# Attention, FFN and gated convolution on one core: the low halves of q and k are subtracted on VectorE instead of GpSimd

## The chip, the cores and the metric

One Trainium2 chip, one of its cores. The metric is the device time of one execution in microseconds (us). The engines have in-order instruction streams: TensorE (PE in the profile, its weight loads PEld), VectorE (DVE), ScalarE (ACT), GpSimd (POOL) and SyncE (SP, which here issues every DMA).

## The reference

Batch 4, 12 heads, sequence 448, head size 64, model width 768, FFN width 3072, all fp32:

```python
scores = scale * q @ k.T - log(S); attn = 1 / (1 + exp(-scores)); x = attn @ v
u = x + real(fft(fft(x, axis=1), axis=2))          # over sequence and width
un = (u - mean(u)) / sqrt(var(u) + 1e-6)
y = u + relu(un @ w_ch1) @ w_ch2
gate = sigmoid(causal_conv5(y)); out = (gate * (y @ w_val)) @ w_out
```

## The kernel before

Every product that needs more than one short-mantissa pass is split in a high and a low half: x = h + l, and a product is taken as three matmuls, h·h, h·l and l·h. For q and k this is done on the chip, in `halves_of` (lines 302 to 310): the high half h is x rounded to fp32r, written by ScalarE (line 308) or, for the first pairs, by VectorE (line 306); the low half l is x − h, one tensor_tensor on GpSimd (line 309).

The attention works on 24 pairs of heads (4 batches of 6). A pair has q of 128 × 448 and k of 128 × 512 (k's last 64 columns are laid out twice, with zeros, so that the fourth tile of keys takes both heads in one matmul). The loop of lines 640 to 695 has 96 passes, t = 0 to 95, four for each pair, one per tile of 128 keys. The order in which a pass issues its work is the order of the code, and each engine keeps it; nothing reorders it:

- `scores(t + 1)` on TensorE (lines 355 and 357), from qh, ql, kh, kl of its pair; it runs one pass ahead. The first score tile of the next pair is thus issued in the pass with t % 4 == 3.
- `sigmoid(t)` on ScalarE.
- In the pass with t % 4 == 0, `prep_q` of the next pair, in the pass with t % 4 == 1 `prep_k`: the high half on ScalarE behind the sigmoid, the low half on GpSimd. The diff touches the second of these. There are 24 ql and 24 kl. Below, ql(t) and kl(t) are those issued in pass t.
- Loads of later q, k, v by SP, and with t % 4 == 2 a maximum over v (line 104, VectorE).
- One step of the background queues, whose VectorE and ScalarE work is issued behind the halves of this pass: `fq`, the Fourier stage of the batch before (lines 400 to 552: sums and differences of x on VectorE, halves ph and pl for the first transform's matmuls of line 464, halves zh and zl of its result for the matmuls of line 481, and additions of the outcome to acc, lines 489 and 492); `lq`, the normalisation of the batch before that (lines 558 to 626); `wq`, the preparation of FFN weights (line 181 on: bit operations on VectorE that turn loaded 64-bit floats into fp32, then maxima and halves). ScalarE work of these queues goes through `push` and `drain` and comes at the pass's end.
- `values(t − 1)` on TensorE (lines 380 and 382), and the copy of a finished pair to acc (line 389).

After the attention, the last batches' Fourier and normalisation run beside the first FFN blocks (`up`, `down`), then come the FFN over eight groups of weights, the gate, and two projections. None of these uses `halves_of`. They have GpSimd work of their own (lines 230, 599, 834), which the diff leaves alone.

Of the kernel before, what the change touches and what calls it, by code (L numbers as in the profile page):

```python
# [7 lines left out]
F32 = mybir.dt.float32  # L8
# [5 lines left out]
ALU = mybir.AluOpType  # L14
# [46 lines left out]
def body(tc, qd, kd, vd, w1d, w2d, cwd, wvd, wod, cdd, k12d, csd, eyed, out):  # L61
    nc = tc.nc
    V, A, P = nc.vector, nc.scalar, nc.gpsimd
# [238 lines left out]
    def halves_of(x, nm, n, on_v):  # L302
        h = wk.tile([128, n], F32R, tag=nm + "h", bufs=2, name=nm + "h")
        l = wk.tile([128, n], F32R, tag=nm + "l", bufs=2, name=nm + "l")
        if on_v:
            V.tensor_copy(h, x)
        else:
            A.activation(out=h, in_=x, func=AF.Copy)
        P.tensor_tensor(out=l, in0=x, in1=h.bitcast(F32), op=ALU.subtract)
        return h, l  # L310

    def prep_q(i):
        qk[i] = halves_of(raw[i][0], "q", S, i == 0)

    def prep_k(i):
        qk[i] += halves_of(raw.pop(i)[1], "k", 512, i < 3)
# [746 lines left out]
```

## Time and profile before

| | |
|---|---|
| time, median of 3 runs | 1081.48 us (1080.37 to 1082.52) |
| profiled execution | 1081.04 us |
| its span, first to last instruction | 1079.2 us |
| mean granted TensorE clock | 0.995 |
| busy: PE, DVE, ACT, POOL | 1058.7, 739.2, 444.4, 180.3 us |

Busy time counts what an engine executes, not what it waits for. The page gives the busy time in whole; the chain that ended last lies in the projections at the end, since every stage hands on to the next. A row of the timeline reads: start, duration, engine, line, operation, output<-inputs, shape, count of merged instructions, and in brackets how long the engine stood idle just before and what ended that.

### The profile page before, as it was taken

To read this page: it belongs to the slowest core of one execution; us is meant where nothing else is said; L and a number is where in the kernel's file an instruction comes from. 1 tells how busy PE (TensorE), PEld (TensorE's weight loads), DVE (VectorE), ACT (ScalarE), POOL (GpSimd) and SP (SyncE) were. 2 spreads that over 40 slices of the span, in tenths; PEclk is the share of its full clock that TensorE was granted. 3 is DMA by queue.
4 is the path that set the end of the run, shared out by engine and by line. 5 is a ranking of instruction groups with operands and counts; after the bars stand their busy time and mean duration, and the time that the engine had idled before them with its cause. 6 is when DMAs were issued, how large, how long until landed. Compare 5 with 4: busy or idle time off the path is not lost. (4 is left out here: it accounts for less than half of the span.)

```text
span 1079.2 us, 15323 instructions
## 1 busy us (share of the span) xinstructions
PE 1058.7 (98%) x5616; PEld 548.9 (51%) x5616; DVE 739.2 (68%) x2143; ACT 444.4 (41%) x686; POOL 180.3 (17%) x162
## 2 busy tenths in 40 slices
PE   9999999999899999999999999999999999999998
PEld 5345454546455555555555555555555545555554
DVE  2866999696985666667676566666666787776530
ACT  5675757732232233333233333133333374444321
POOL 3322223200020112211021122012221061000000
PEclk9999999999999999999999999999999999999999
DMA  6632432011112322223322222322222200000001
GB/s 218 211 94 88 130 97 88 11 46 45 30 30 59 83 64 69 78 60 88 89 75 72 60 74 72 89 73 60 73 71 76 60 1 1 1 35 35 35 35 69
DMA packets 34780, 74.13 MB, mean 69 GB/s; under 512 B 3940, under 2 KB 11920, under 8 KB 34704
## 3 DMA queue, kind: packets, MB, share of 16 engines
q1 hardware_dynamic: 34704, 73.15, 23.7%
q8 instruction: 44, 0.72, 0.3%
q14 instruction: 32, 0.26, 0.1%
HBM read 67.46 MB, written 5.51 MB: 68 GB/s over the span
## 5 line engine op out<-in xcount | busy, mean ns | idle before, releaser
L730 PE MATMUL ps_s<-un,w1hi 128*128 128x448 f16 x1152 | 312.8, 353 | 2.0 <-DVE hl L739 2.0
L753 PE MATMUL ps_m<-hh,w2hi 128*128 128x448 f16 x576 | 203.5, 353 | 3.6 <-DVE acc L757 2.4
L753 PE MATMUL ps_m<-hh,w2lo 128*128 128x448 f16 x576 | 203.6, 353 | 0.0
L753 PE MATMUL ps_m<-hl,w2hi 128*128 128x448 f16 x576 | 203.4, 353 | 0.0
L730 PE MATMUL ps_s<-un,w1lo 128*128 128x448 f16 x576 | 203.4, 353 | 0.0
L753 PEld LDWEIGHTS <-w2hi 128*128 128x128 f16 x1152 | 112.4, 98 | 109.4 <-issue 5.0
L730 PEld LDWEIGHTS <-w1hi 128*128 128x128 f16 x1152 | 112.9, 98 | 108.3 <-issue 4.1
L757 DVE SCALAR_TENSOR_TENSOR acc<-ps_m,rg,acc 128x448 f32<-128x448 f32 x192 | 129.1, 680 | 36.8 <-PE ps_m L753 36.6
L178 ACT ACTIVATE wabs<-w 128x384 f32<-128x384 f32 (+1 forms) x109 | 58.4, 547 | 223.9 <-DMA w<-w2d 81.1
L739 DVE SCALAR_TENSOR_TENSOR hl<-ps_s,hh 128x896 f16<-128x896 f32 x64 | 54.7, 855 | 80.0 <-ACT hh L737 79.9
L189 DVE TENSOR_SCALAR_CACHE_REDUCE wabs<-wabs 128x192 f32<-128x192 f32 (+1 forms) x234 | 74.7, 354 | 41.7 <-ACT wabs L178 40.7
L368 ACT ACTIVATE sg<-ps_s,logb 128x896 f32<-128x896 f32 x96 | 86.5, 912 | 26.8 <-PE ps_s L355 22.6
L753 PEld LDWEIGHTS <-w2lo 128*128 128x128 f16 x576 | 56.4, 98 | 53.0 <-issue 0.7
L730 PEld LDWEIGHTS <-w1lo 128*128 128x128 f16 x576 | 56.5, 98 | 52.8 <-issue 0.4
L191 DVE TENSOR_SCALAR wf<-wabs 128x192 int32<-128x192 int32 (+1 forms) x234 | 54.4, 272 | 35.6 <-POOL w1lo L230 13.2
L929 PE MATMUL ps_m<-xs,wvhi 128*128 128x448 f16 x288 | 78.0, 352 | 0.0
L197 DVE SCALAR_TENSOR_TENSOR wf<-w,wf 128x192 int32<-128x192 int32 (+1 forms) x234 | 77.3, 369 | 0.3
L737 ACT ACTIVATE hh<-ps_s 128x896 f16<-128x896 f32 x64 | 46.1, 720 | 73.6 <-PE ps_s L730 73.6
L194 DVE SCALAR_TENSOR_TENSOR wf<-w,wf 128x192 int32<-128x192 int32 (+1 forms) x234 | 74.6, 357 | 0.3
L380 PE MATMUL ps_m<-sg,v 128*64 128x448 f32 x288 | 70.3, 568 | 0.0
L810 DVE SCALAR_TENSOR_TENSOR gp<-acc,cw,gp 128x448 f32<-128x448 f32 x72 | 49.3, 685 | 20.3 <-ACT gp L808 18.4
L954 PE MATMUL ps_m<-gh,wohi 128*128 128x448 f16 x144 | 50.8, 352 | 0.0
(185 smaller groups left out, 1399.1 us busy)
## 6 DMA issues: line engine op xcount, KB each, us to landing
w<-w1d SPq DMA_DIRECT2D x42, 384.0 KB
w<-w2d SPq DMA_DIRECT2D x42, 384.0 KB
k<-kd SPq DMA_DIRECT2D x24, 256.0 KB
v<-vd SPq DMA_DIRECT2D x24, 256.0 KB
q<-qd SPq DMA_DIRECT2D x24, 224.0 KB
out<-o SPq DMA_DIRECT2D x24, 224.0 KB
w<-wvd SPq DMA_DIRECT2D x12, 384.0 KB
w<-wod SPq DMA_DIRECT2D x12, 384.0 KB
```

Source lines behind the costliest of these rows:

```text
L178: A.activation(out=wa, in_=z[:, :, 1].bitcast(F32), func=AF.Abs)
L189: V.tensor_scalar(out=a, in0=a, scalar1=LEAST, scalar2=None, op0=ALU.max, op1=ALU.max, accum_out=m[:, i:i + 1])
L191: V.tensor_scalar(out=f.bitcast(I32), in0=a.bitcast(I32), scalar1=0x07FFFFFF, scalar2=3, op0=ALU.bitwise_and, op1=ALU.logical_shift_left)
L194: V.scalar_tensor_tensor(out=f.bitcast(I32), in0=lo, scalar=29, in1=f.bitcast(I32), op0=ALU.logical_shift_right, op1=ALU.bitwise_or)
L197: V.scalar_tensor_tensor(out=f.bitcast(I32), in0=hi, scalar=-0x40000000, in1=f.bitcast(I32), op0=ALU.bitwise_and, op1=ALU.bitwise_or)
L368: A.activation(out=sg[:, :n], in_=sc.pop(t)[:, :n, :S], func=AF.Sigmoid, scale=1.0 / math.sqrt(D), bias=logb)
L380: nc.tensor.matmul(p[hs, :S], v[:, s, hs], a[:, h], start=(s == 0), stop=False)
L730: nc.tensor.matmul(p[:, i, :S], w[:, k, fs], u[:, k], start=(m == 0), stop=(m == 17))
L739: V.scalar_tensor_tensor(out=l[:, :nf], in0=p[:, :nf, :S], scalar=0.0, in1=h[:, :nf], op0=ALU.max, op1=ALU.subtract)
L753: nc.tensor.matmul(p[:, :S], w[:, f, js], hh[f // 2][k][:, f % 2], start=(m == 0), stop=(m == 3 * FC - 1))
L757: V.scalar_tensor_tensor(out=acc[b][:, j, PAD:], in0=p[:, :S], scalar=rg, in1=acc[b][:, j, PAD:], op0=ALU.mult, op1=ALU.add)
L929: nc.tensor.matmul(p[:, :S], w[:, k, js], u[:, k], start=(n == 0), stop=(n == 17))
```

## The change

One line: the subtraction that makes the low half is issued on VectorE's stream in place of GpSimd's. Operands, shapes, place in the code and everything around it are the same.

```diff
@@ halves_of
             V.tensor_copy(h, x)
         else:
             A.activation(out=h, in_=x, func=AF.Copy)
-        P.tensor_tensor(out=l, in0=x, in1=h.bitcast(F32), op=ALU.subtract)
+        V.tensor_tensor(out=l, in0=x, in1=h.bitcast(F32), op=ALU.subtract)
         return h, l
```

## Rows read from the trace of the kernel before

**Rows 1.** The page, busy time and share of each engine.
```profile
PE 1058.7 (98%) x5616; PEld 548.9 (51%) x5616; DVE 739.2 (68%) x2143; ACT 444.4 (41%) x686; POOL 180.3 (17%) x162
```

**Rows 2.** Busy time by stretch: stretch, length, PE, PEld, DVE, ACT, POOL; clock, DMA.
```profile
105.00:148.00 43.00, 41.87 (x220) 19.81 (x220) 41.94 (x85) 29.41 (x44) 14.05 (x11) 1.00 0.43 127
164.00:196.00 32.00, 30.14 (x156) 13.56 (x152) 31.12 (x60) 23.92 (x36) 9.95 (x8) 1.00 0.25 74
232.00:300.00 68.00, 60.62 (x323) 34.59 (x322) 57.74 (x159) 19.42 (x29) 2.75 (x3) 0.95 0.14 36
```

**Rows 3.** Line 309: duration min/median/max in ns; what ended POOL's idle time.
```profile
L309 POOL TENSOR_TENSOR ql<-q,qh x24: 1135/1144/1957, 3.8 to 202.3; 128x448 fp32r<-128x448 f32 x24
L309 POOL TENSOR_TENSOR kl<-k,kh x24: 1265/1284/1703, 5.3 to 208.4; 128x512 fp32r<-128x512 f32 x24
  ACT qh L308: 88.5, 22
```

**Rows 4.** DVE groups of 105 to 148 us: operation, shapes, count, busy us, mean ns.
```profile
L104 DVE TENSOR_REDUCE vm<-v 128x1 f32<-128x512 f32 x5 | 3.4, 678 | 0.0
L398 DVE TENSOR_TENSOR pm<-acc 128x448 f32<-128x448 f32 x2 | 1.1, 611 | 0.0
```

**Rows 5.** Timeline, 25 to 37 us: passes 7 to 15.
```profile
25.16 0.69 DVE L181 TENSOR_SCALAR wabs<-w 128x256 int32<-128x256 int32 x1 [9.70 <-DMA w<-w1d]
...
26.01 0.36 PE L355 MATMUL ps_s<-qh,kl 64*128 64x448 f32 x2
...
27.13 0.42 DVE L197 SCALAR_TENSOR_TENSOR wf<-w,wf 128x256 int32<-128x256 int32 x1
...
36.27 0.47 PE L355 MATMUL ps_s<-qh,kh 64*128 64x448 f32 x2 [1.90 <-ACT sg L368]
```

**Rows 6.** Timeline, 66 to 93 us: passes 32, 33, 41 and 42.
```profile
66.56 0.68 DVE L450 SCALAR_TENSOR_TENSOR e<-eo,st,e 12x452 f16<-12x452 f32 x1
67.29 0.92 DVE L436 SCALAR_TENSOR_TENSOR pl<-pm,st,ph 128x678 f16<-128x678 f32 x1
68.05 0.56 ACT L308 ACTIVATE qh<-q 128x448 fp32r<-128x448 f32 x1
70.04 0.66 PE L464 MATMUL ps_m<-cd,pl 128*113 128x385 f16 x3
90.64 0.63 ACT L308 ACTIVATE kh<-k 128x512 fp32r<-128x512 f32 x1
91.78 0.62 DVE L456 SCALAR_TENSOR_TENSOR zl<-ps_m,rt,zh 112x385 fp32r<-112x385 f32 x1 [4.54 <-ACT zh L259]
92.44 0.09 PEld L481 LDWEIGHTS ps_m<-cs,zl 112*6 112x6 f32 x1 [0.38 <-DVE zl L456]
```

**Rows 7.** Passes 45 to 62: the stretch 99.5 to 104.3, then timeline rows.
```profile
99.50:104.30 4.80, 4.80 (x32) 2.74 (x29) 4.13 (x17) 1.97 (x4) 0.00 (x0) 1.00 0.16 48
...
103.66 0.63 ACT L308 ACTIVATE kh<-k 128x512 fp32r<-128x512 f32 x1
...
109.03 2.76 DVE L564 TENSOR_TENSOR tt<-tt,acc 128x448 f32<-128x448 f32 x3
...
113.11 0.37 PE L355 MATMUL ps_s<-qh,kl 64*128 64x448 f32 x2
...
136.38 1.05 DVE L585 TENSOR_TENSOR tt<-tt 128x448 f32<-128x448 f32 x1
...
138.15 0.95 PE L596 MATMUL ps_m<-ones,tt 128*112 128x1 f32 x8 [0.18 <-DVE tt L587]
```

**Rows 8.** Timeline, 148 to 174 us: passes 65, 66 and 72.
```profile
148.46 0.63 ACT L308 ACTIVATE kh<-k 128x512 fp32r<-128x512 f32 x1
...
151.10 0.28 PE L481 MATMUL ps_m<-cs,zl 112*6 112x256 f32 x1
...
171.89 0.37 PE L355 MATMUL ps_s<-qh,kl 64*128 64x448 f32 x2
...
172.31 1.95 DVE L564 TENSOR_TENSOR tt<-tt,acc 128x448 f32<-128x448 f32 x3
```

## The prediction, as put on record before the run

> **What bounds the kernel now.** I read the busy times first. TensorE is busy 98% of the span, VectorE 68%, GpSimd 17% [rows 1]: an engine that is relieved here gains nothing by itself, and what counts is only whether TensorE gets its operands earlier or later. Next the busy times by stretch. The diff acts in the attention alone, and there the averages mislead: from 105 to 148 us VectorE is busy 41.94 of 43 us and from 164 to 196 us 31.12 of 32, while TensorE loses 1.13 and 1.86 us [rows 2]. In these stretches VectorE is as full as TensorE. Then line 309: GpSimd takes 1.14 us for a ql and 1.28 for a kl, and waited 88.5 us for qh in 22 of its 24 ql [rows 3]. It does nothing else there, so each low half starts the moment its high half is out, and whatever VectorE is doing. Last the timeline, beside the code's order of issue, for the question that a share of busy time can't answer: where VectorE's stream stands when the high half comes. That decides, because on VectorE the subtraction has a place in a queue: if VectorE is early it must wait there for ScalarE, with everything queued behind; if it is late, TensorE waits for the subtraction.
>
> **What goes and what comes.** 24 ql and 24 kl leave GpSimd. On VectorE the nearest row is the fp32 tensor_tensor of line 398, two SBUF inputs, 128 × 448, 0.611 us, and for 512 columns 0.68 (the reduction of line 104 over 128 × 512 takes 0.678) [rows 4]. Added: 24 × 0.61 + 24 × 0.68 = 31 us of VectorE work. The bounds are these and GpSimd's own durations, which would make 58; the operation of the same kind on the same engine is the nearer row.
>
> Something comes back. Three chained tensor_tensors of line 564 take 1.95 us at 172.31, but 2.76 at 109.03, where GpSimd runs a ql [rows 7, 8]; line 585 takes 1.05 at 136.38 in place of 0.61 [rows 4, 7]. VectorE instructions that meet line 309 on GpSimd are held up, and that ends. From 104.8 to 138 us there are seven such, the first in these rows 0.8 and the last 0.4, together about 5.2 us. So in the full stretches the work on VectorE stays about level. What doesn't stay is the order, and the sum is made of that, place by place. The cost at each is how much later TensorE gets what it already waits for, or gets just in time.
>
> *Passes 7 to 9 (late).* VectorE stands 9.70 us for a load of weights until 25.16; kl(9) lies behind the conversion that follows, whose last instruction ends at 27.13 + 0.42 = 27.55 [rows 5]. With ql(8) at 0.6 in between and 0.6 of hold-ups gone, kl(9) ends at 27.55 + 0.68 = 28.2. TensorE reads it at 26.01: 2.2 us late. TensorE then idles 1.90 before 36.27, for a sigmoid that sits behind a load [rows 5]; that load isn't moved, so this idle time covers 1.9. Left: 0.3. Without the cover it is 2.2.
>
> *Passes 32 and 80 (early).* VectorE would come to ql(32) at 66.5 and wait for qh, which ends at 68.05 + 0.56 = 68.61. Behind it stand line 450 (0.68) and pl (0.92), so pl ends at 68.61 + 0.61 + 0.68 + 0.92 = 70.8; TensorE takes it at 70.04 [rows 6]. 0.8 us; the same three stand behind ql(80). Together 1.6.
>
> *Passes 41, 65 and 89 (early).* kh(41) ends at 90.64 + 0.63 = 91.27. Then kl 0.68, the first zl 0.62, line 104 0.68, the second zl 0.62: 93.87, where TensorE's weight load now waits for it until 92.44 [rows 4, 6]. 1.4 us. The same chain of 2.6 us follows two more times; there it has 2.0 us, from 148.46 + 0.63 = 149.09 to 151.10 [rows 8]: 0.6 each. Together 2.6.
>
> *Pass 45 and the full stretch.* kh(45) ends at 103.66 + 0.63 = 104.29, kl(45) at 104.97. Between 99.5 and 104.3 VectorE did 4.13 us of work [rows 7] that is queued behind kl(45) in the code. So it is 4.8 us late at the start of a stretch in which it has 1.1 us to spare [rows 2]. The first to feel it is kl(49), wanted at 113.11. Up to 138 come four ql and three kl, 4.5 us; the hold-ups give 5.2 back, idle time some 0.7: 4.8 + 4.5 − 5.2 − 0.7 = 3.4. At 138.15 TensorE starts a matmul that waited for VectorE [rows 7], so all of it arrives: 3.4 us. Bounds: nothing, if the hold-ups give twice as much, and 4.8.
>
> *Pass 73.* kl(73) is queued behind the first of the line 564 instructions that start at 172.31, but TensorE reads kl at 171.89 [rows 8]: even on the old schedule VectorE gets there too late, by 172.31 + 0.65 + 0.68 − 171.89 = 1.8, plus its lateness from kl(69) and less the hold-ups. Bounds 0 and 4.8; I take 2.0.
>
> Sum: 0.3 + 1.6 + 2.6 + 3.4 + 2.0 = 9.9 us. Between these places VectorE waits for ScalarE again, which is shifted with TensorE, so the terms add; what falls inside one full stretch I counted once. After the attention TensorE is idle 7.4 us of 232 to 300, but VectorE is busy 57.74 of the 68 [rows 2]: that idle time ends on VectorE, which is shifted too, and covers nothing. From 300 us on nothing is touched. The profiled execution took 1081.04 us, 0.44 under the median: 1081.04 + 9.9 = 1090.9, and 1091 against the median.
>
> **The rivals.** *Faster:* the hold-ups are what counts. If VectorE's results reach TensorE earlier for that, most of what TensorE loses in the two full stretches goes, 1.13 + 1.86 = 3.0 us [rows 2], and the time is 1078. It decides where VectorE is late and no low half is wanted soon. For it: a VectorE subtraction is half of GpSimd's [rows 3, 4], and the full stretches get about as much back as they get in. Against it: three of the places above are early waits, which no shorter instruction removes, and kl(9) and kl(73) stand behind work that TensorE doesn't need.
>
> The Trainium skill speaks for this rival: GPSIMD Engine Reference, section 4.1 Engine selection, sends elementwise work on a tile to VectorE and calls GpSimd about twice as slow for two inputs. The price agrees with the trace, 1.14 against 0.61 us; followed as a rule it gives the 1078, because it prices the instruction and not its place in the queue.
>
> *No change:* the loop has slack that I don't see at these places (a matmul that doesn't need the late operand first), and the losses stay under 2 us: 1081. For it: ql, by its place, has a pass more than kl, and no place above depends on ql alone. Against it: at 92.44 and 138.15 TensorE already stands waiting [rows 6, 7].
>
> *Much slower:* ScalarE's stream has the same weakness. An activation of the Fourier or normalisation stage that waits for a late VectorE result keeps the next sigmoid behind it, and TensorE waits for that. I counted none of these. If each of the two full stretches is hit with the whole 4.8 in place of 3.4 and 2.0, and the uncovered 1.9 of passes 7 to 9 comes on top, that is 9.9 + 1.4 + 2.8 + 1.9 = 16, 1097. The same follows if a VectorE subtraction costs nearer to 1 us.
>
> **How the numbers follow.** Forecast, slower by 5 to 13 us: 0.56. Much slower: 0.18. No change: 0.12. Faster: 0.14. About 0.2%, 2 us, is what a measurement tells from no change. Slower by more than that is 0.56 + 0.18 and a little of the third case goes to it, 0.76; within 0.2% 0.10; faster 0.14. The range leaves out most of the faster case and the tail of the heavy one: 1079.5 to 1098. The forecast alone would be 1086 to 1094.
>
> **What would show it.** Right: the attention's end comes some 10 us later, and everything behind it is shifted and otherwise equal; VectorE's waits list ql and kl waiting for qh and kh, some 20 to 30 us in total; TensorE waits for kl of line 309 near pass 11; the TensorE idle time before 36 us is gone; TensorE waits longer for zl and pl. VectorE's lines 564, 181, 191 and 197 have their short durations everywhere. Wrong: TensorE's idle time in the attention is no longer than now, or the loss lies after it.

## The result and the profile after

| | before | after |
|---|---|---|
| time, median of 3 runs | 1081.48 us | 1091.48 us (1091.39 to 1093.04) |
| ratio | | 1.0106, 95% interval 1.009 to 1.0122 |
| profiled execution | 1081.04 us | 1091.48 us |
| its span | 1079.2 us | 1089.7 us |

The change costs 1.06%, some 10 us, where 9.9 us were forecast. The first row is the page of the changed kernel; it answers to [rows 1].

```profile
PE 1060.4 (97%) x5616; PEld 548.2 (50%) x5616; DVE 743.4 (68%) x2191; ACT 444.8 (41%) x686; POOL 119.9 (11%) x114
```

GpSimd lost its 48 instructions and 60 us. VectorE got the same 48, but its busy time grew by 4.2 us only: 31 us of subtractions came, so by the difference about 27 us of hold-ups went. Nothing in these totals says slower.

The next rows are line 309 of the changed kernel: duration min/median/max in ns, and what ended VectorE's idle time before it (us, count). They answer to [rows 3].

```profile
L309 DVE TENSOR_TENSOR ql<-q,qh x24: 612/619/626, 3.6 to 213.9; 128x448 fp32r<-128x448 f32 x24
L309 DVE TENSOR_TENSOR kl<-k,kh x24: 681/691/693, 4.6 to 220.0; 128x512 fp32r<-128x512 f32 x24
  ACT kh L308: 25.5, 12
  ACT qh L308: 19.6, 10
```

A subtraction is half as long as on GpSimd. But VectorE now stands 45.1 us in front of 22 of the 48, waiting for ScalarE. GpSimd waited longer and nobody was queued behind it.

The same stretches of the changed kernel as in [rows 2], with the same columns. Each kernel's stretches are cut by its own time, so they do not hold exactly the same work:

```profile
105.00:148.00 43.00, 39.47 (x194) 17.77 (x195) 39.77 (x101) 29.12 (x42) 0.15 (x1) 0.96 0.34 105
164.00:196.00 32.00, 28.99 (x143) 12.94 (x140) 27.19 (x69) 18.48 (x27) 0.00 (x0) 0.95 0.26 75
232.00:300.00 68.00, 59.94 (x330) 34.24 (x330) 59.17 (x167) 20.25 (x30) 1.06 (x2) 0.99 0.16 43
```

In the first two, TensorE does 194 and 143 matmuls in place of 220 and 156 and now loses 3.5 and 3.0 us; VectorE is less full than before, and the granted clock has fallen to 0.96 and 0.95. VectorE has idle time and TensorE is later all the same: the loss is one of order. In the third stretch the clock is better than before, 0.99 against 0.95; that comes back below.

**Where the time went.** Both traces hold 5616 matmuls in the same order. So the start of the nth matmul after, less its start before, is the lateness of TensorE at that place, whatever it does between. It is the measure for all that follows. Places are given by the time before.

| place | forecast | lateness after it | its part |
|---|---|---|---|
| start (first pair) | not counted | −1.2 | −1.2 |
| passes 7 to 16 | 0.3 | −0.6 | +0.5 |
| between, to 69 us | – | −0.4 | +0.3 |
| pass 32 | 0.8 | +0.6 | +1.0 |
| pass 41 | 1.4 | +1.9 | +1.3 |
| passes 45 to 62 | 3.4 | +6.0 | +4.1 |
| pass 65, and 0.5 behind it | 0.6 | +7.3 | +1.3 |
| pass 73 | 2.0 | +10.2 | +2.9 |
| pass 80 | 0.8 | +11.6 | +1.4 |
| pass 89 | 0.6 | +12.1 | +0.5 |
| after the attention | 0 | +10.5 | −1.6 |

The rows behind it, from the timeline of the changed kernel (start, duration, engine, line, output<-inputs, idle time before and what ended it):

```profile
26.46 0.68 DVE L309 TENSOR_TENSOR kl<-k,kh 128x512 fp32r<-128x512 f32 x1
27.20 0.47 PE L355 MATMUL ps_s<-qh,kl 64*128 64x448 f32 x2 [2.20 <-DVE kl L309]
...
68.29 0.62 DVE L309 TENSOR_TENSOR ql<-q,qh 128x448 fp32r<-128x448 f32 x1 [2.11 <-ACT qh L308]
70.62 0.70 PE L464 MATMUL ps_m<-cd,pl 128*113 128x385 f16 x3 [0.78 <-DVE pl L436]
...
91.94 0.69 DVE L309 TENSOR_TENSOR kl<-k,kh 128x512 fp32r<-128x512 f32 x1 [4.40 <-ACT kh L308]
94.33 0.29 PE L481 MATMUL ps_m<-cs,zl 112*6 112x256 f32 x1 [1.32 <-DVE zl L456]
...
106.20 0.69 DVE L309 TENSOR_TENSOR kl<-k,kh 128x512 fp32r<-128x512 f32 x1 [3.91 <-ACT kh L308]
115.99 0.68 DVE L309 TENSOR_TENSOR kl<-k,kh 128x512 fp32r<-128x512 f32 x1
116.72 0.47 PE L355 MATMUL ps_s<-qh,kl 64*128 64x448 f32 x2 [1.58 <-DVE kl L309]
...
144.40 0.95 PE L596 MATMUL ps_m<-ones,tt 128*112 128x1 f32 x8 [0.45 <-DVE tt L587]
...
180.97 0.68 DVE L309 TENSOR_TENSOR kl<-k,kh 128x512 fp32r<-128x512 f32 x1
181.71 0.52 PE L355 MATMUL ps_s<-qh,kl 64*128 64x448 f32 x2 [2.35 <-DVE kl L309]
...
197.28 0.70 PE L464 MATMUL ps_m<-cd,pl 128*113 128x385 f16 x3 [0.77 <-DVE pl L436]
200.01 0.97 PE L380 MATMUL ps_m<-sg,v 128*64 128x448 f32 x4 [1.03 <-DVE un L582]
```

Two kinds of row are to be told apart. At 68.29, 91.94 and 106.20 VectorE is early: the bracket stands at the subtraction, and the work queued behind it reaches TensorE late (pl, zl, and at 116.72 the next kl). At 26.46, 115.99 and 180.97 the subtraction has no bracket: VectorE comes to it late, and TensorE has the bracket. Each of the three late ones is followed by a stretch at a lower granted clock (columns as above):

```profile
28.00:32.00 4.00, 4.00 (x12) 1.33 (x9) 3.72 (x11) 1.45 (x2) 0.00 (x0) 0.57 0.92 277
116.00:122.00 6.00, 5.28 (x21) 2.21 (x22) 5.97 (x12) 1.88 (x3) 0.00 (x0) 0.72 0.47 139
180.00:186.00 6.00, 4.29 (x15) 1.72 (x16) 5.93 (x11) 1.47 (x2) 0.00 (x0) 0.72 0.44 129
```

The length of a stretch by what is missing in the clock gives 4 × 0.43 = 1.7, 6 × 0.28 = 1.7 and again 1.7 us, about as much as the waits themselves. But the kernel before has such stretches too. Between 10 and 1070 us it has three (clock 0.57 from 37 to 41 us, 0.72 from 238 to 244, 0.59 from 286 to 290). The changed kernel has the three above and a fourth (0.57 from 298 to 302), so in the end the clock makes a difference of one stretch.

### The profile page after: what moved, and what is told of

Its sections match the earlier page's. It is cut to its first block, busy times and chain, and to the rows that moved or that the text cites. A ratio compares the mean times of both kernels' runs of the same rounds, so it can differ in the third digit from the quotient of the medians.

```text
span 1089.7 us, 15286 instructions
## 1 busy us (share of the span) xinstructions
PE 1060.4 (97%) x5616; PEld 548.2 (50%) x5616; DVE 743.4 (68%) x2191; ACT 444.8 (41%) x686; POOL 119.9 (11%) x114
## 4 chain that ended last, share of the span: by engine, by line
PE 82%; DVE 11%; ACT 3%; issue 1%; DMA 1%; SPq 0%; DVEq 0%; ACTq 0%
PE ps_m L753 27%; PE ps_s L730 27%; PE ps_m L929 8%; PE ps_m L954 8%; PE ps_m L380 3%; PE ps_s L355 3%; PE ps_m L481 2%; PE ps_m L382 1%; PE ps_m L464 1%; DMA w<-w1d 1%; ACT sg L368 1%; DVE un L582 1%; PE ps_s L357 1%; DVE acc L757 1%; DVE kl L309 1%
## 5 line engine op out<-in xcount | busy, mean ns | idle before, releaser
L191 DVE TENSOR_SCALAR wf<-wabs 128x192 int32<-128x192 int32 (+1 forms) x234 | 51.0, 256 | 35.1 <-POOL w1lo L230 13.7
L194 DVE SCALAR_TENSOR_TENSOR wf<-w,wf 128x192 int32<-128x192 int32 (+1 forms) x234 | 74.2, 355 | 0.2
L197 DVE SCALAR_TENSOR_TENSOR wf<-w,wf 128x192 int32<-128x192 int32 (+1 forms) x234 | 74.1, 354 | 0.2
L954 PE MATMUL ps_m<-gl,wohi 128*128 128x448 f16 x144 | 50.8, 353 | 0.0
```

The lines of the kernel that those rows point to most:

```text
L194: V.scalar_tensor_tensor(out=f.bitcast(I32), in0=lo, scalar=29, in1=f.bitcast(I32), op0=ALU.logical_shift_right, op1=ALU.bitwise_or)
L197: V.scalar_tensor_tensor(out=f.bitcast(I32), in0=hi, scalar=-0x40000000, in1=f.bitcast(I32), op0=ALU.bitwise_and, op1=ALU.bitwise_or)
L954: nc.tensor.matmul(p[:, :S], w[:, k, js], gs[b, k][i], start=(n == 0), stop=(n == 17))
```

## The experiments

Each ratio is against the kernel before on the same chip (1080.2 to 1081.2 us).

**Wait and work apart.** *wait_only*: GpSimd keeps the subtraction; at its place VectorE copies one column of the high half into a scratch that nobody reads, so it waits there and does next to nothing.

```diff
         P.tensor_tensor(out=l, in0=x, in1=h.bitcast(F32), op=ALU.subtract)
+        V.tensor_copy(w1, h[:, n - 1:n].bitcast(F32))
```

> The subtractions stay on GpSimd. VectorE gets, at the place where the changed kernel has the subtraction, a copy of one column of the high half: the wait for ScalarE without the work. Queue theory (it is the place in VectorE's stream that costs): the early places are paid, about 0.3 us at pass 32, 0.8 at pass 41, 3 to 4 from pass 45 on, nothing at passes 9 and 73, where kl comes from GpSimd again: 4 to 6 us slower than before, 1085 to 1088. Work theory (the 31 us of VectorE work cost): 48 copies of under 0.1 us are 4 us of 740, no change, within 1 us of before.

*work_only*: GpSimd keeps the subtraction; VectorE does one of the same size that waits for no high half, into a scratch.

```diff
         P.tensor_tensor(out=l, in0=x, in1=h.bitcast(F32), op=ALU.subtract)
+        V.tensor_tensor(out=d[:, :n], in0=x, in1=x, op=ALU.subtract)
```

> The subtractions stay on GpSimd. VectorE gets, at the same places, a subtraction of the same size of the raw tile from itself into scratch that nobody reads: the work without the wait for ScalarE. Queue theory: nothing at the early places (passes 32, 41, 80, 89); in the full stretches 11 us of work come in and the hold-ups stay, so up to 4 us there: 0 to 5 us slower than before. Work theory: as slow as the changed kernel or slower, 10 us or more, because here the hold-ups by GpSimd stay.

Measured: wait_only 1093.21 us, 1.0121 (1.0106 to 1.0136); work_only 1097.09, 1.0159 (1.014 to 1.0178). That the wait alone costs nothing is refuted: 24 × 2 copies of 0.147 us, some 7 us of work in all, cost 13 us. But the size was more than twice what I had expected. And work_only came out as the other theory had it: I had expected 0 to 5 us, it costs 17, and that theory said 10 or more. These two runs alone do not decide between wait and work. Rows of wait_only, from its line 311, its timeline and what it waited for:

```profile
L311 DVE COPY w<-qh x24: 140/147/156, 3.7 to 214.2; 128x1 f32<-128x1 f32 x24
  ACT qh L308: 19.8, 9
  ACT kh L308: 17.7, 7
```
```profile
107.57 0.15 DVE L311 COPY w<-kh 128x1 f32<-128x1 f32 x1 [4.38 <-ACT kh L308]
...
127.03 0.67 ACT L259 ACTIVATE e<-eo,st 12x452 f16<-12x452 f32 x1 [4.59 <-DVE eo L419]
128.41 0.74 PE L357 MATMUL ps_s<-qh,kh 64*128 64x448 f32 x2 [3.00 <-ACT sg L370]
```

and of work_only, the added subtraction, the same two engines, and the stretch from 105 us:

```profile
L311 DVE TENSOR_TENSOR dm<-q x24: 607/618/1559, 3.6 to 215.8; 128x448 f32<-128x448 f32 x24
```
```profile
69.59 0.67 ACT L259 ACTIVATE e<-eo,st 12x452 f16<-12x452 f32 x1 [3.63 <-DVE eo L419]
70.97 0.47 PE L357 MATMUL ps_s<-qh,kh 64*128 64x448 f32 x2 [2.68 <-ACT sg L370]
```
```profile
105.00:148.00 43.00, 38.66 (x195) 18.07 (x193) 42.10 (x92) 26.39 (x39) 11.52 (x8) 0.96 0.32 96
```

Both hold the route that the prediction named under "much slower" and left uncounted: an activation of the Fourier stage (line 259) waits 4.59 or 3.63 us for VectorE, the sigmoid stands behind it on ScalarE, and TensorE waits 3.00 or 2.68 us for the sigmoid. In the lateness these are 4.6 of wait_only's 11.0 us and 3.6 of work_only's 14.4. Both figures hold the lower clock behind the wait. The second kernel also keeps GpSimd's hold-ups (one of its own subtractions took 1.559 us) beside full VectorE stretches, so it is no clean price for the work; how its 17 us divide between work, hold-ups and this route is not shown. early_high, below, has the work without the waits.

**One tensor alone.** *ql_only* and *kl_only*:

```diff
-        P.tensor_tensor(out=l, in0=x, in1=h.bitcast(F32), op=ALU.subtract)
+        (V if nm == "q" else P).tensor_tensor(out=l, in0=x, in1=h.bitcast(F32), op=ALU.subtract)
```

> Only ql goes to VectorE, kl stays on GpSimd. Queue theory: the places of ql are passes 32 and 80, 0.8 us each, and little in the full stretches: 1 to 3 us slower than before. Work theory: half of the work, so half of the loss, 4 to 5 us slower.

> Only kl goes to VectorE, ql stays on GpSimd. Queue theory: the places of kl are passes 9, 41, 45, 65, 73 and 89, which hold most of the loss: 7 to 9 us slower than before. Work theory: half of the work, 4 to 5 us slower.

Measured: ql_only 1086.92, 1.0061 (1.0041 to 1.008); kl_only 1091.0, 1.0102 (1.0084 to 1.0119). kl is the dearer one, as its place says, but both are dearer than either theory had it, and 6.8 + 10.8 = 17.6 us is more than the 10 us of both together. Each keeps half of GpSimd's work, and so part of the hold-ups; how the excess divides I did not settle. One row of ql_only's timeline, where TensorE at [rows 7] waited 0.18:

```profile
141.79 0.95 PE L596 MATMUL ps_m<-ones,tt 128*112 128x1 f32 x8 [1.48 <-DVE tt L587]
```

ql, of which the prediction said under "no change" that no place depends on it alone (against its own passes 32 and 80), makes VectorE late at the end of the full stretch. With the lower clock behind it (0.66 from 143 to 148 us) this one place makes 2.6 of the 6.5 us of lateness that ql_only ends with.

**The wait taken away.** *early_high*: the changed kernel, with only the high halves made a pass sooner on ScalarE; every low half stays at its place on VectorE. *early_high_pool*: the same with the low halves on GpSimd.

```diff
+        if t % 4 == 0 and t // 4 + 1 < NPAIR:
+            high_k(t // 4 + 1)
+        if t % 4 == 3 and t // 4 + 2 < NPAIR:
+            high_q(t // 4 + 2)
```

> As the changed kernel, but ScalarE makes the high halves one pass earlier (qh with t % 4 == 3, kh with t % 4 == 0); the subtractions stay on VectorE at their places. So the waits for ScalarE go and the work stays. Queue theory: passes 32, 41, 45, 65, 80 and 89 cost nothing any more, passes 9 and 73, where VectorE is late, still do: 0 to 4 us slower than before, 1080 to 1084. Work theory: the work is that of the changed kernel, and so is the time, 1091.

> The control for the one above: the same earlier high halves, with the subtractions on GpSimd as before. Both theories: GpSimd was never late with a low half, so within 2 us of before.

Measured: early_high 1075.25, 0.9948 (0.9933 to 0.9962); early_high_pool 1078.37, 0.9979 (0.997 to 0.9988). Both are faster than expected: 1080 to 1084 for the first, within 2 us of before for the second, which gains 2.5. Line 312, the subtraction, and its waits in early_high, then two rows of its timeline, and the two full stretches:

```profile
L312 DVE TENSOR_TENSOR ql<-q,qh x24: 608/620/626, 3.7 to 195.1; 128x448 fp32r<-128x448 f32 x24
  ACT qh L308: 5.1, 6
  ACT kh L308: 2.0, 3
```
```profile
27.13 0.47 PE L370 MATMUL ps_s<-qh,kl 64*128 64x448 f32 x2 [1.21 <-DVE kl L312]
...
168.10 0.47 PE L370 MATMUL ps_s<-qh,kl 64*128 64x448 f32 x2 [0.29 <-DVE kl L312]
```
```profile
105.00:148.00 43.00, 43.00 (x235) 21.89 (x234) 40.26 (x97) 31.63 (x47) 1.18 (x1) 1.00 0.41 127
164.00:196.00 32.00, 31.26 (x165) 15.04 (x166) 30.67 (x65) 26.48 (x39) 1.01 (x1) 1.00 0.22 65
```

All the work of the change is there, VectorE's waits have gone from 45.1 to 7.1 us, the late places have shrunk (1.21 and 0.29 in place of 2.20 and 2.35), and from 105 to 148 us TensorE has no idle time. That the work itself makes the changed kernel slower falls with this. With GpSimd in its place the same stretch has TensorE at 41.03 of 43 us:

```profile
105.00:148.00 43.00, 41.03 (x219) 19.99 (x217) 41.53 (x81) 29.83 (x44) 13.79 (x10) 1.00 0.41 125
```

So with the waits gone, moving the subtraction gains 3.1 us, close to the price that the "faster" rival had set (3.0). The lateness between the two profiled executions says where: 2.4 us by the end of the attention, and these from 105 to 148 us. The rest comes behind the attention, net of several jumps; there early_high_pool has two stretches at a lower clock (0.57 from 236 to 240 us and from 284 to 288), and early_high has none (1.00 from 230 to 300). That the subtraction makes this part is not shown. Early_high is faster than the kernel before by 0.52% and than the changed one by 1.6%, the best version here.

*wait_early*: early_high_pool with wait_only's copies.

> The control for the kernel that waited without the work: subtractions on GpSimd, the one-column copies on VectorE, but the high halves a pass earlier, so that the copies have nothing to wait for. Queue theory: the 48 copies of 0.15 us cost little by themselves, 1078 to 1082, some 12 us faster than the same copies with their waits. If the copies themselves cost, 1088 or more.

Measured: 1078.77, 0.9976 (0.9965 to 0.9988). The same 48 copies that cost 13 us where the high half is late cost 0.4 us (against early_high_pool) where it is mostly ready: their waits fall from 37.5 to 6.6 us. That is the cleanest pair of this study: same instructions, same place on VectorE, and what differs is when the high half is made. The profiles put it less sharply. By the end of the attention the copies have cost 11.9 us in wait_only, against the kernel before, and 2.1 in wait_early, against early_high_pool, of which 1.7 are one stretch at a lower clock (0.66 from 46 to 51 us); behind the attention wait_early has no such stretch where early_high_pool has two.

*early_both*: the changed kernel with the low halves one pass earlier as well, and the high halves a pass ahead of these.

> Subtractions on VectorE one pass earlier than in the changed kernel (ql with t % 4 == 3, kl with t % 4 == 0), high halves on ScalarE one pass ahead of these. Queue theory: now VectorE may also be late by a pass, so passes 9 and 73 get cheaper too, and the hold-ups by GpSimd are gone: 3 us faster to 2 us slower than before. Work theory: 1091.

Measured: 1076.65, 0.996 (0.9946 to 0.9974). That is more than the 3 us gained at best that I had expected, but no better than early_high. From this alone it does not follow that an earlier subtraction brings nothing. In its trace (of its slowest execution, 1079.99 us) the wait for kl(9) is gone, and TensorE gains 1.4 us on early_high there. But the second pair's qh now stands ahead of the first sigmoid on ScalarE: TensorE waits 2.30 us for that sigmoid at 10.15, the clock is 0.57 from 10 to 14 us, and from there it is 3.5 us behind early_high. VectorE also waits 17.6 us for qh, in 8 places. What an earlier subtraction alone is worth is not shown.

**Single places.** *one_wait*: the changed kernel, in which kh(45) alone is made one pass earlier.

```diff
+        if t == 44:
+            high_k(t // 4 + 1)
```

> The changed kernel with one of its 48 waits taken away: only kh(45) is made a pass earlier on ScalarE, in pass 44. Queue theory: VectorE enters the full stretch behind pass 45 some 4 us less late, so of the 4.1 us that the changed kernel loses between passes 45 and 62 (TensorE stood 1.9 us behind the kernel before at 105 us of that trace, 6.0 us at 145) 3 to 4 go: 1087 to 1089. Work theory: one instruction moved by a pass changes nothing, 1091.

Measured: 1088.89, 1.007 (1.0057 to 1.0082). Its timeline where the changed kernel waited 3.91 us, and the stretch that answers to 116 to 122 us above:

```profile
98.83 0.62 ACT L308 ACTIVATE kh<-k 128x512 fp32r<-128x512 f32 x1
...
101.82 0.69 DVE L312 TENSOR_TENSOR kl<-k,kh 128x512 fp32r<-128x512 f32 x1
```
```profile
116.00:122.00 6.00, 6.00 (x31) 2.58 (x29) 5.52 (x13) 3.61 (x6) 0.00 (x0) 1.00 0.49 132
```

The subtraction has no wait, the clock is whole, and passes 45 to 62 cost 0.8 us in place of 4.1. One wait of the 22 makes 3.3 us of the lateness at that place, as the prediction's fourth step had it.

*first_pair*: the kernel before, with ql and kl of the first pair alone on VectorE.

> The kernel before, but ql and kl of the first pair alone go to VectorE, where no wait for ScalarE lies behind them because VectorE makes these high halves itself. In the changed kernel TensorE's first score matmuls stand 1.2 us earlier. Expected: 1 us faster than before if that reaches the end, under what can be told for certain.

Measured: 1079.92, 0.9991 (0.9983 to 1.0). The median is 1 us lower, as expected, but this is within what can be told from no change, and the lateness of its profile is +0.4 through the attention and −0.5 only at the end. Nor is there a gain at the start that could reach the end: at 9 us its lateness is −0.1, where the changed kernel has −1.2. The part on what stood outside the sum comes back to this.

## Why the prediction was right, point by point

**Not the work but the order.** Shown. The four corners, as ratios to the kernel before:

| | high half as before | high half a pass earlier |
|---|---|---|
| low half on GpSimd | 1 | 0.9979 |
| low half on VectorE | 1.0106 | 0.9948 |

On VectorE the order is worth 0.0158, 17 us; on GpSimd 2 us. In the Trainium skill, PSUM — Partial Sum Buffer, section Engine vs sequencer instructions, the queues of ScalarE, VectorE and GpSimd are strict FIFO (first in, first out). The trace agrees, and wait_only against wait_early is that rule with a price.

**The subtraction's price.** 0.61 and 0.68 us were taken; 0.619 and 0.691 measured. That the hold-ups give back about as much as comes in also held: 4.2 us more VectorE busy time for 31 us added. Line 564, 0.95 us a piece in its four from 105 to 148 us before (3.8 us), and line 585 are at their short durations after (105 to 155 us, columns as [rows 4]):

```profile
L564 DVE TENSOR_TENSOR tt<-tt,acc 128x448 f32<-128x448 f32 x4 | 2.5, 620 | 0.1
L585 DVE TENSOR_TENSOR tt<-tt 128x448 f32<-128x448 f32 x3 | 1.8, 614 | 0.0
```

**Passes 7 to 9.** 2.2 us late was forecast, TensorE waited 2.20. The cover was there too, and the net part was 0.5 for 0.3. Both sides were larger than counted: the wait brings 1.7 us of lower clock, and the idle time that it covers had brought some as well, as this row of the kernel before shows, behind [rows 5]:

```profile
38.00:40.00 2.00, 2.00 (x9) 0.99 (x10) 1.90 (x7) 1.99 (x5) 1.14 (x1) 0.50 0.55 160
```

The idle time of 1.90 us before the matmul at 36.27 is gone in the changed kernel, as was said: there that matmul starts at 37.15 without a wait.

**Passes 32, 41 and their like.** 0.8 and 1.4 were forecast; 1.0 and 1.3 came, with the chain as described (pl and zl). Pass 89 has 0.5 for 0.6. Pass 65 has 0.7 more than forecast, most of it behind the pass, and pass 80 0.6 more, for there TensorE waits 1.03 us for a line that I had not looked at (line 582's un, which holds a PSUM buffer that the matmul of line 380 needs).

**Pass 45 and the full stretch.** The cause held, by one_wait. The route failed: the step said that the lateness arrives with the matmul that was at 138.15 and that kl(49) is only the first to feel it. It arrived with kl(49): 1.58 us of wait and 1.7 of clock, 3.3 of the 4.1 us, and at the later place the wait grew from 0.18 to 0.45 only.

**Pass 73.** Mis-sized: 2.0 for 2.9. The wait was 2.35 us, by which the lateness grew by 2.5; the lower clock added 1.6, and 1.2 came back about 10 us later, where the kernel before had idle time of its own:

```profile
182.41 0.47 PE L355 MATMUL ps_s<-qh,kh 64*128 64x448 f32 x2 [1.16 <-ACT sg L368]
```

**What stood outside the sum.** Three terms, and they nearly cancel. The clock was never counted, though the row at 38 us showed it. The start was not counted. And "covers nothing" of the idle time after the attention was wrong by 1.6 us. The rows of both kernels, the start before, then after:

```profile
2.69 3.41 PE L283 MATMUL ps_m<-ones 128*128 128x128 f32 x15
...
5.26 1.27 POOL L309 TENSOR_TENSOR kl<-k,kh 128x512 fp32r<-128x512 f32 x1 [0.36 <-DVE kh L306]
```
```profile
2.70 2.70 PE L283 MATMUL ps_m<-ones 128*128 128x128 f32 x15
...
4.61 0.69 DVE L309 TENSOR_TENSOR kl<-k,kh 128x512 fp32r<-128x512 f32 x1
```

VectorE has the first kl at 5.30, GpSimd at 6.53. But the 15 matmuls of line 283, which the change does not touch, took 3.41 us in the one execution and 2.70 in the other: TensorE was quicker from the start, and only so could it use the earlier kl. In first_pair the 15 matmuls take 3.41 us again, VectorE has kl at 5.42, and nothing is gained. In early_high_pool they take 2.55 us, and TensorE waits 0.87 us for GpSimd's kl. The gain needs both. The change makes only one of them, so the 1.2 us are in part luck of the profiled execution; why TensorE starts quicker in some is not shown.

TensorE after the attention, before (with a stretch that follows it), then after:

```profile
237.73 0.54 PE L730 MATMUL ps_s<-un,w1hi 128*128 128x448 f16 x2 [1.99 <-DVE hl L739]
...
240.00:244.00 4.00, 4.00 (x17) 2.25 (x16) 3.96 (x11) 0.43 (x1) 0.00 (x0) 0.70 0.26 53
```
```profile
249.72 0.54 PE L730 MATMUL ps_s<-un,w1hi 128*128 128x448 f16 x2 [1.93 <-DVE hl L739]
```

The idle time itself did stay, 1.99 and 1.93 us: the argument that it ends on VectorE held. What went is the low clock behind it (0.70 from 240 to 244 us before; 1.00 from 249 to 256 after). Why an idle time of the same length is followed by it in one kernel and not in the other is open.

**The rivals.** *Faster* failed for the reason given against it, and its mechanism is real: some 2.4 us in the attention once the waits are gone. *No change* fell with the 45.1 us of waits. *Much slower*: the ScalarE route exists, and decided part of wait_only and work_only; in the changed kernel none of the large jumps of the lateness goes through it. Of the signs, 20 to 30 us for VectorE's waits was too low: 45.1 were measured. The short durations came: lines 564, 181 and 191 took up to 1.444, 1.826 and 1.240 us before and at most 0.627, 0.298 and 0.295 after.

Of the 9.9 us, then, the places are read from the two traces, and that the order in VectorE's queue makes them is shown, at pass 45 by removing the one wait and for all of them together by early_high. That the sum matches to a few tenths is luck: terms of both signs that I left out nearly cancel.

## What to carry to other kernels

A cheap instruction that is moved to a busy engine is priced by its place in that engine's queue: ask what stands behind it when its operand is late, and who wants it when the engine is late. If the move is wanted, make its operand earlier first; here that turned +1.1% into −0.5%. And a wait of TensorE of 2 us is to be counted with the clock behind it, which here nearly doubled it at three places; behind a fourth, of 1.93 us after the attention, no lower clock came.

## What the runs showed of the hardware

The hold-ups are selective. At 91.78 [rows 6] a VectorE instruction with one operand in PSUM ran in 0.62 us beside a GpSimd subtraction that lasted from 91.34 to 92.62. Line 564 with two SBUF inputs took 0.95 on the mean from 105 to 148 us, and one of work_only's subtractions 1.559 in place of 0.618. The rows of the kernel before, the second one the durations of line 181 (min/median/max in ns):

```profile
91.34 1.28 POOL L309 TENSOR_TENSOR kl<-k,kh 128x512 fp32r<-128x512 f32 x1 [4.61 <-ACT kh L308]
```
```profile
L181 DVE TENSOR_SCALAR wabs<-w x18: 279/286/1826, 25.2 to 159.7; 128x256 int32<-128x256 int32 x18
```

The Trainium skill, SBUF — State Buffer, section SBUF: two separate sides, says that VectorE instructions with two SBUF inputs, or in a mode that uses two ports, and GpSimd shut each other out for a whole instruction. For two inputs the rows agree. Line 181 has one input and is held up as well, up to 1.826 us where the changed kernel has at most 0.298, so two inputs are not the whole condition; whether it runs in such a mode no row here shows.
